# Gated linear attention and a routed MLP: scores in two 64-column halves of the array, several levels per piece

## The chip, the cores and the metric

The kernel runs on one core of one Trainium2 chip. The metric is the device time in microseconds of one execution. All data are fp32 in memory. TensorE (PE) multiplies, PEld is its weight load, DVE is VectorE, ACT is ScalarE, POOL is GpSimd, and SP is the engine whose queue issues most DMAs.

## What is computed

```python
# attention: q, k, v, alpha of shape (4, 8, 768, 48)
for t in range(S):
    state = alpha[:, :, t, :, None] * state + np.einsum('bhd,bhe->bhde', k[:, :, t], v[:, :, t])
    y[:, :, t] = np.einsum('bhd,bhde->bhe', q[:, :, t], state)
# bridge: x = y as (3072, 384); then E = 4 experts, F = 1024
p = domain_probs / (domain_probs.sum(-1, keepdims=True) + 1e-09)
for e in range(E):
    h = np.maximum(x @ w1[e], 0.0)
    out += p[:, e:e + 1] * (h @ w2[e])
```

## The kernel before

**Units and groups.** The 768 steps of a batch row are cut into 6 chunks of 128; a unit is one chunk of one of the 4 batch rows, so there are 24 units. A unit's 128 rows are also 128 tokens of the MLP. Units form seven groups: group 0 has two units, groups 1 to 5 four each, group 6 two. While the MLP of group g runs, the attention of group g+1 is mixed into it, piece by piece; the two units of group 0 run at the start with nothing but filler matmuls (`fill`, L569) beside them.

**A unit of attention** (`attention`, L254) is a generator; each `yield` ends a piece. Pieces 0 to 2 turn alpha, k and q so that head features lie on the partitions, two heads (64 rows each) per tile of 128, four such pairs. The decays between two steps of a chunk are products of alphas; they are applied in seven levels, m = 1, 2, 4, ..., 64. At level m the chunk is cut into blocks of 2m steps, and the scores of keys in the first half of a block with queries in its second half are final. So at each level:

- `next_q` (L290) copies the 64 queries of the second halves to a block `qb` on ACT, two copies, one for each head of a pair, so that the other head's rows of the block stay zero. Then DVE multiplies those queries in QT by the decay of the half before them, and forms the next level's decays `dec`.
- L317: four matmuls, one per pair of heads, with K (128 features x 128 keys) as the stationary operand and `qb` (2 heads x 64 queries) as the moving one. Scores `sc` are 128 keys x 8 heads x 64 queries. From m = 32 on, the last keys are left off (96 and 64 columns).
- L325: DVE multiplies the keys of the first halves, in place in KT, by the decay of the half behind them. As it is in place, it waits until the level's matmuls have read KT.
- the valid part of `sc` goes into `lat`, the unit's 128 x 128 matrix per head: for m up to 16 by a predicated copy on DVE under a mask (L334), for 32 and 64 by three plain copies on ACT (L330).

The diagonal of `lat` is q.k of the same step, written by eight ACT instructions (L272), each a scaled identity. There are two `lat` tiles. Then come `yps` (L352), scores times values plus queries times the old state, on 32 array columns each; the turned K (L369); and the state's update (L373 to L382).

**The MLP.** `up` (L396) computes one of 8 column blocks of 128 of x @ w1; `down` (L454) multiplies one unit's h by w2 in 8 steps. An expert is 8 `up` and then one `down` per unit of the group. Weights come in four pieces (chunks c = 0 to 3) per expert and layer, two `up` per chunk. A weight may be split into three fp32r parts, which multiply faster; the split parts are made once on ACT and DVE (`split_piece`, L199, driven by `background`, L213) and written to DRAM (`kept`), in group 0 for w1 and in group 1 for w2. Later groups load the 1152 KB of a `kept` piece; w1 is unsplit in group 0 (and for chunk 3 of group 6), w2 is unsplit in groups 0, 1 and 6:

```python
    split1 = lambda gi, e, c=0: gi > 0 and (gi < len(groups) - 1 or c < NQ - 1)
    split2 = lambda gi, e, c=0: 1 < gi < len(groups) - 1
```

`load_piece` (L173) issues the load of a piece on SP's queue, which runs in order and waits for the tile to be free. An unsplit piece of 384 KB goes into a `w_raw` tile or into the third part of a `w2` tile. w2 of the next expert is ordered at the end of the last `down` (L503 to L508): two chunks at once and two, `late`, after the first chunk's `up` (L445). `hidden[c]` (L403) is the tile `hT` of a chunk, three parts x 2 column blocks x up to 512 tokens; with unsplit w2 only its third part holds h (L412).

**What sets the order.** The program is written in the order in which each engine runs it. `attend` (L518) gives each unit's pieces a due beat (`BEATS`, L137; units follow one another by 6.5 beats), and `advance` (L538) is called after each `up` and within `down` with an estimated cost (L512), and runs the pieces that are due. For the two units at the start the order is written out by hand (L575, L582).

[...]

## Time and profile before

| | us |
|---|---|
| median of 3 runs | 1161.94 (1161.48 to 1162.81) |
| the profiled execution | 1161.86, of which the span 1160.1 |
| PE busy | 1131.0 (97%) |
| DVE busy | 759.0 (65%) |
| ACT busy | 556.5 (48%) |
| group 0: first `up` to the first of group 1 | 30 to 190 |
| group 6: first `up` to the end | 1078 to 1160 |

HBM reads are 229.8 MB and writes 42.5 MB, 235 GB/s over the span. The granted PE clock is full nearly everywhere after the start. A line of the page such as "x1344 | 180.8, 278 | 16.7" gives the number of instructions, their busy time in us, the mean of one in ns, and the engine's idle time just ahead of them. Matmul records overlap in the pipeline, so the sum of their durations is more than the time that they hold PE; the distance from one start to the next is what counts. An fp32 matmul leaves two matmul records and two weight-load records, an fp32r matmul one of each.

### The profile page before, as it was taken

The numbers are of one execution on the slowest core, as the hardware profiler recorded it, in microseconds if no ns is written. First come the engines' busy times: TensorE is split into PE (matmuls) and PEld (weight loads), VectorE is DVE, ScalarE is ACT, GpSimd is POOL, SyncE is SP. The second block draws the span as 40 slices with busy tenths as digits, with TensorE's granted clock in tenths as the row PEclk, the third lists the DMA queues.
The fourth block names the chain that finished last, engine by engine and source line by source line (L and its number), as shares of the span: only waits on it lengthen the run. The fifth ranks groups of instructions, "written<-read, shape, count | busy, mean of one in ns | idle before, by whom it ended". The sixth has DMA issues, their size and how long they took to land.

```text
span 1160.1 us, 19270 instructions
## 1 busy us (share of the span) xinstructions
PE 1131.0 (97%) x7354; PEld 960.2 (83%) x7354; DVE 759.0 (65%) x1450; ACT 556.5 (48%) x1215; POOL 34.4 (3%) x73
## 2 busy tenths in 40 slices
PE   8789999999999999999999999999999999999998
PEld 8677777686767798998898988989988998998875
DVE  5557755566565868686778695786885777557211
ACT  6557745645636546444456353464462356223221
POOL 1000000000000100000000000000000000000000
PEclk9989999999999999999999999999999999999999
DMA  7657669775767949557749385776493787458783
GB/s 145 215 171 255 203 195 321 263 266 186 251 232 242 395 131 341 170 192 301 263 164 315 127 273 215 258 256 247 132 326 126 294 299 300 169 199 353 236 312 92
DMA packets 166188, 273.54 MB, mean 236 GB/s; under 512 B 120624, under 2 KB 140976, under 8 KB 142032
## 3 DMA queue, kind: packets, MB, share of 16 engines
q1 hardware_dynamic: 156704, 230.06, 57.7%
q0 software_dynamic: 6016, 42.08, 9.1%
q8 instruction: 59, 0.97, 0.3%
q10 hardware_dynamic: 3376, 0.17, 0.2%
q14 instruction: 33, 0.27, 0.1%
HBM read 229.81 MB, written 42.47 MB: 235 GB/s over the span
## 4 chain that ended last, share of the span: by engine, by line
PE 81%; DVE 8%; DMA 4%; ACT 4%; issue 2%; SPq 0%; POOL 0%; ACTq 0%; DVEq 0%; POOLq 0%
PE one L424 17%; PE ops L480 13%; PE sc L317 11%; PE two L424 8%; PE ops L475 7%; PE ops L478 7%; PE ops L476 7%; PE yps L352 4%; PE tp L251 3%; PE one L416 2%; DMA w<-in_moe_w_dram 2%; DVE hT L229 2%; DVE t L430 2%; PE sps L373 1%; DVE hT L233 1%
## 5 line engine op out<-in xcount | busy, mean ns | idle before, releaser
L424 PE MATMUL one<-xT,w 128*128 128x512 f32 (+1 forms) x1104 | 278.5, 387 | 0.9 <-DMA w<-kept 0.9
L424 PEld LDWEIGHTS one<-xT,w 128*128 128x128 f32 x1104 | 191.8, 188 | 37.6 <-issue 2.6
L428 ACT ACTIVATE t<-one 128x512 f32<-128x512 f32 (+1 forms) x184 | 104.9, 570 | 225.6 <-PE one L424 166.8
L317 PEld LDWEIGHTS sc<-qb,KT 128*128 128x128 f32 (+2 forms) x1344 | 168.6, 181 | 44.3 <-ACT qb L297 15.6
L317 PE MATMUL sc<-qb,KT 128*128 128x128 f32 (+2 forms) x1344 | 180.8, 278 | 16.7 <-ACT qb L297 10.1
L475 PE MATMUL ops<-w,hT 128*128 128x384 f32 x512 | 180.7, 353 | 0.0
L297 ACT COPY qb<-QT 64x256 f32<-64x256 f32 x336 | 136.5, 406 | 78.8 <-DVE QT L301 48.2
L478 PE MATMUL ops<-w,hT 128*128 128x384 f32 x512 | 173.1, 338 | 0.4
L476 PE MATMUL ops<-w,hT 128*128 128x384 f32 x512 | 172.6, 337 | 0.0
L424 PE MATMUL two<-xT,w 128*128 128x512 f32 (+1 forms) x552 | 148.6, 377 | 0.0
L480 PE MATMUL ops<-w_raw,hT 128*128 128x384 f32 x384 | 130.8, 487 | 0.0
L325 DVE TENSOR_TENSOR KT<-KT,dec 128x256 f32<-128x256 f32 x144 | 60.8, 422 | 96.3 <-PE sc L317 95.0
L430 DVE TENSOR_TENSOR t<-t,two 128x512 f32<-128x512 f32 x128 | 87.7, 685 | 51.1 <-PE two L424 32.6
L424 PEld LDWEIGHTS two<-xT,w 128*128 128x128 f32 x552 | 100.3, 188 | 19.8
L334 DVE COPY_PREDICATED lat<-masks,sc 128x512 f32<-128x512 uint8 x120 | 113.8, 948 | 0.2
L480 PEld LDWEIGHTS ops<-w_raw,hT 128*128 128x128 f32 x384 | 70.4, 190 | 41.8 <-issue 0.9
L475 PEld LDWEIGHTS ops<-w,hT 128*128 128x128 f32 x512 | 96.3, 188 | 3.3 <-issue 2.8
L478 PEld LDWEIGHTS ops<-w,hT 128*128 128x128 f32 x512 | 96.0, 188 | 2.2 <-DVE hT L233 2.0
L476 PEld LDWEIGHTS ops<-w,hT 128*128 128x128 f32 x512 | 96.4, 188 | 0.2
L233 DVE SCALAR_TENSOR_TENSOR hT<-hT 128x512 fp32r<-128x512 f32 x128 | 88.6, 692 | 4.4
L229 DVE SCALAR_TENSOR_TENSOR hT<-t,hT 128x512 fp32r<-128x512 f32 x128 | 87.6, 684 | 0.0
L226 ACT ACTIVATE hT<-t 128x512 fp32r<-128x512 f32 x128 | 80.3, 627 | 10.4 <-DVE t L430 9.1
(79 smaller groups left out, 1146.3 us busy)
## 6 DMA issues: line engine op xcount, KB each, us to landing
w<-kept SPq DMA_DIRECT2D x156, 1152.0 KB
kept<-w POOLq DMA_DIRECT2D x32, 1152.0 KB, 6.5
w_raw<-in_moe_w_dram SPq DMA_DIRECT2D x32, 384.0 KB
w_raw<-in_moe_w_dram SPq DMA_DIRECT2D x48, 128.0 KB
w<-in_moe_w_dram SPq DMA_DIRECT2D x16, 384.0 KB
ra<-in_alpha_dram SPq DMA_DIRECT2D x23, 192.0 KB
rk<-in_k_dram SPq DMA_DIRECT2D x23, 192.0 KB
rq<-in_q_dram SPq DMA_DIRECT2D x23, 192.0 KB
```

Source lines behind the costliest of these rows:

```text
L229: nc.vector.scalar_tensor_tensor(out=low, in0=x, scalar=0.0, in1=top.bitcast(F32), op0=ALU.max, op1=ALU.subtract)
L233: nc.vector.scalar_tensor_tensor(out=dif, in0=top.bitcast(F32), scalar=1 / 4096.0, in1=low.bitcast(F32), op0=ALU.mult, op1=ALU.subtract)
L297: nc.scalar.copy(out=qb[rows, :, i, :].rearrange("p a (b r) -> p a b r", r=m), in_=qv[rows])
L317: nc.tensor.matmul(sc[:past, 2 * p:2 * p + 2, :].rearrange("p i r -> p (i r)"), lhsT=KT[:, p, :past], rhs=qb[:, p].rearrange("p i r -> p ( ...
L334: nc.vector.copy_predicated(halves(lat, m)[:, :, :, 1, :], mk.unsqueeze(1).broadcast_to([P, H, nb, m]), sc.rearrange("p a (b r) -> p a b r ...
L424: nc.tensor.matmul(out, lhsT=w[:, part, kc], rhs=xTs[gi][:, part, kc, :n], start=(part == terms[0] and kc == 0), stop=(part == terms[-1] a ...
L428: nc.scalar.activation(out=t, in_=one, func=ACT.Copy, scale=FINE)
L430: nc.vector.tensor_sub(t, t, two)
L475: nc.tensor.matmul(sums[0], lhsT=h[:, 1], rhs=w[:, 1], start=(fc == 0), stop=False)
L476: nc.tensor.matmul(sums[0], lhsT=h[:, 0], rhs=w[:, 0], start=False, stop=(fc == FCH - 1))
L478: nc.tensor.matmul(sums[1], lhsT=h[:, 2], rhs=w[:, 2], **ends)
L480: nc.tensor.matmul(sums[0], lhsT=h[:, 2].bitcast(F32), rhs=w, **ends)
```

## The change

Five things are done together.

1. For levels 1 to 32, keys and queries are taken in two halves of 64 steps. Per pair of heads there are two matmuls, each with 64 keys as stationary columns and 2 x 32 queries as moving ones; their outputs lie on partitions 0 to 63 and 64 to 127, so in two halves of the array's columns. Level 64 has keys of the first half and queries of the second alone: four matmuls with 64 stationary and 128 moving columns, two of them in each half of the columns, into `far`.
2. Levels 1 to 8 are multiplied in one piece, levels 16, 32 and 64 in another. For this K of each level has its own tile (five rotate): ACT copies the second halves of the blocks to the new tile, and DVE writes the first halves times the decay. There are four `qb` blocks in place of three.
3. Scores within a half are collected in `near` (128 x 8 x 64), whose diagonal is one DVE product of a stacked identity with `dot` in place of eight ACT instructions. The predicated copies have 32 columns per head in place of 64. Level 32 goes into `near` by two ACT copies, `far` into `lat` by two, `near` into `lat` by two. There is one `lat` tile, whose lower left quarter is zeroed once.
4. An unsplit w2 piece is loaded into the unused first part of its chunk's `hT` tile, ordered when the chunk's first `up` begins; unsplit w1 always goes to the third part of a `w2` tile. The `w_raw` tiles are gone.
5. A unit still has 14 pieces, now at beats 0 to 13, and the order at the start is written anew.

```diff
-    j = np.arange(P)[:, None]
-    n = np.arange(HALF)[None, :]
-    mask_np = np.stack(
-        [(j // (2 * m) == n // m) & (j % (2 * m) < m) for m in LEVELS], 1).astype(np.uint8)
-    ident_np = np.eye(P, dtype=np.float32)
+    j = np.arange(P)[:, None] % HALF
+    n = np.arange(QUAD)[None, :]
+    mask_np = np.stack([(j // (2 * m) == n // m) & (j % (2 * m) < m) for m in LEVELS[:5]],
+                       1).astype(np.uint8)
+    ident_np = np.concatenate([np.eye(P), np.tile(np.eye(HALF), (2, 1))], 1).astype(np.float32)
...
-    ident = const.tile([P, P], F32, name="ident")
-    masks = const.tile([P, len(LEVELS), HALF], U8, name="masks")
+    ident_all = const.tile([P, P + HALF], F32, name="ident")
+    ident = ident_all[:, :P]
+    masks = const.tile([P, 5, QUAD], U8, name="masks")
...
-    lats = [const.tile([P, H, P], F32, name=f"lat{i}") for i in range(2)]
+
+    near = const.tile([P, H, HALF], F32, name="near")
+    lat = const.tile([P, H, P], F32, name="lat")
...
-    blocks = [const.tile([P, NP, 2, HALF], F32, name=f"qb{i}") for i in range(3)]
+    blocks = [const.tile([P, NP, 2, HALF], F32, name=f"qb{i}") for i in range(4)]
...
-    BEATS = [0, 1, 2, 2.5, *range(3, 13)]
+    BEATS = list(range(14))
...
-    def load_piece(l, i):
+    def load_piece(l, i, beside=False):
...
-        if l == 1 and gi == 0 or l == 0 and gi > 0:
+        if l == 1 and not beside:
+            return
+        if l == 0:
+
             w = wts.tile([P, 3, KC * QF], F32R, name="w2", bufs=NQ)[:, 2].bitcast(F32)
         else:
-            w = wts.tile([P, KC * QF], F32, name="w_raw", bufs=NQ)
+
+            w = hidden[c][:, 0].rearrange("p f n -> p (f n)")[:, :KC * QF].bitcast(F32)
         wt[l][i] = w
...
-        lat = lats[u % 2]
         pair = lambda t: lambda p: t[:, 2 * p:2 * p + 2, :].rearrange("p b c -> p (b c)")
+        keys = lambda: work.tile([P, NP, P], F32, name="KT", bufs=5)
 
         AT = work.tile([P, NP, P], F32, name="AT")
-        KT = work.tile([P, NP, P], F32, name="KT")
         QT = work.tile([P, NP, P], F32, name="QT")
         nc.scalar.copy(out=AT, in_=turned(pair(ra)))
-
...
-        def diagonals(which):
-            for h in which:
-                nc.scalar.activation(out=lat[:, h, :], in_=ident, func=ACT.Copy,
-                                     scale=dot[:, h:h + 1])
...
         decs = [AT]
+        KTs = [KT]
+        qbs = []
         spread = lambda t, m: t.unsqueeze(3).broadcast_to([*t.shape, m])
         halved = lambda t: t.rearrange("p a (b two) -> p a b two", two=2)
 
-        def next_q(li):
-
+        def copy_q(li):
             m = LEVELS[li]
             qv = halves(QT, m)[:, :, :, 1, :]
             qb = free.popleft()
+            qbs.append(qb)
             for i in range(2):
                 rows = slice(HD * i, HD * (i + 1))
                 nc.scalar.copy(out=qb[rows, :, i, :].rearrange("p a (b r) -> p a b r", r=m),
                                in_=qv[rows])
-            yield qb
+
+        def next_q(li):
+            m = LEVELS[li]
+            qv = halves(QT, m)[:, :, :, 1, :]
             dv = halved(decs[li])
             nc.vector.tensor_mul(qv, qv, spread(dv[:, :, :, 0], m))
-            dec = work.tile([P, NP, P // (2 * m)], F32, name=f"dec{li}")
+            dec = work.tile([P, NP, P // (2 * m)], F32, name=f"dec{li}", bufs=1)
             nc.vector.tensor_mul(dec, dv[:, :, :, 0], dv[:, :, :, 1])
             decs.append(dec)
 
-        ahead = next_q(0)
-        coming = next(ahead)
-        next(ahead, None)
-        yield
-        for li, m in enumerate(LEVELS):
-            nb = P // (2 * m)
-            qb = coming
-            sc = ps.tile([P, H, HALF], F32, name="sc", tag="sc")
-            wide = m >= 32
-            past = P - m if wide else P
+        def next_k(li):
+            m = LEVELS[li]
+            old = new = halves(KTs[li], m)
+            if li + 1 < len(LEVELS):
+                KTs.append(keys())
+                new = halves(KTs[-1], m)
+                nc.scalar.copy(out=new[:, :, :, 1, :], in_=old[:, :, :, 1, :])
+            nc.vector.tensor_mul(new[:, :, :, 0, :], old[:, :, :, 0, :],
+                                 spread(halved(decs[li])[:, :, :, 1], m))
+
+        def products(li, out):
+
             for p in range(NP):
-                nc.tensor.matmul(sc[:past, 2 * p:2 * p + 2, :].rearrange("p i r -> p (i r)"),
-                                 lhsT=KT[:, p, :past],
-                                 rhs=qb[:, p].rearrange("p i r -> p (i r)"),
+                for s in range(2):
+                    nc.tensor.matmul(
+                        out[HALF * s:HALF * (s + 1), 2 * p:2 * p + 2, :],
+                        lhsT=KTs[li][:, p, HALF * s:HALF * (s + 1)],
+                        rhs=qbs[li][:, p, :, QUAD * s:QUAD * (s + 1)], start=True, stop=True)
+            free.append(qbs[li])
+
+        def take(li, scores):
+            m = LEVELS[li]
+            nb = HALF // (2 * m)
+            mk = masks[:, li, :].rearrange("p (b r) -> p b r", r=m)
+            nc.vector.copy_predicated(
+                near.rearrange("p a (b two r) -> p a b two r", two=2, r=m)[:, :, :, 1, :],
+                mk.unsqueeze(1).broadcast_to([P, H, nb, m]),
+                scores.rearrange("p a (b r) -> p a b r", r=m))
+
+        def scores():
+            return ps.tile([P, 2, H, QUAD], F32, name="sc", tag="sc")
+
+        for li in range(3):
+            copy_q(li)
+            next_q(li)
+            next_k(li)
+            if li == 1:
+
+                nc.vector.tensor_mul(near, ident_all[:, P:].unsqueeze(1).broadcast_to([P, H, HALF]),
+                                     dot.unsqueeze(2).broadcast_to([P, H, HALF]))
+            if li == 2:
+                copy_q(3)
+            yield
+        banks = [scores() for _ in range(2)]
+        for li in range(4):
+            products(li, banks[li // 2][:, li % 2])
+        next_q(3)
+        next_k(3)
+        copy_q(4)
+        take(0, banks[0][:, 0])
+        take(1, banks[0][:, 1])
+        yield
+        next_q(4)
+        next_k(4)
+        copy_q(5)
+        take(2, banks[1][:, 0])
+        take(3, banks[1][:, 1])
+        yield
+        next_q(5)
+        next_k(5)
+        copy_q(6)
+        yield
+        bank = scores()
+        far = ps.tile([P, NP // 2, 2, HALF], F32, name="far", tag="sc")
+        for li in (4, 5):
+            products(li, bank[:, li - 4])
+
+        for r in range(NP // 2):
+            for s in range(2):
+                nc.tensor.matmul(far[HALF * s:HALF * (s + 1), r],
+                                 lhsT=KTs[6][:, 2 * r + s, :HALF], rhs=qbs[6][:, 2 * r + s],
                                  start=True, stop=True)
-            free.append(qb)
-            ahead = next_q(li + 1) if li + 1 < len(LEVELS) else iter(())
-            coming = next(ahead, None)
-            kv = halves(KT, m)[:, :, :, 0, :]
-            nc.vector.tensor_mul(kv, kv, spread(halved(decs[li])[:, :, :, 1], m))
-            if wide:
-
-                for blk in range(nb):
-                    rows = slice(2 * m * blk, 2 * m * blk + m)
-                    nc.scalar.copy(out=lat[rows, :, 2 * m * blk + m:2 * m * (blk + 1)],
-                                   in_=sc[rows, :, m * blk:m * (blk + 1)])
-            else:
-                mk = masks[:, li, :].rearrange("p (b r) -> p b r", r=m)
-                nc.vector.copy_predicated(
-                    halves(lat, m)[:, :, :, 1, :],
-                    mk.unsqueeze(1).broadcast_to([P, H, nb, m]),
-                    sc.rearrange("p a (b r) -> p a b r", r=m))
-            next(ahead, None)
-            yield
+        free.append(qbs[6])
+        next_q(6)
+        next_k(6)
+        take(4, bank[:, 0])
+        for s in range(2):
+            rows = slice(HALF * s, HALF * s + QUAD)
+            nc.scalar.copy(out=near[rows, :, QUAD:], in_=bank[rows, 1])
+        yield
+        parts = lat.rearrange("p (r s i) c -> p r s i c", s=2, i=2)
+        for s in range(2):
+            rows = slice(HALF * s, HALF * (s + 1))
+            nc.scalar.copy(out=parts[:HALF, :, s, :, HALF:], in_=far[rows])
+        for s in range(2):
+            rows = slice(HALF * s, HALF * (s + 1))
+            nc.scalar.copy(out=lat[rows, :, rows], in_=near[rows])
+        KT = KTs[-1]
+        yield
 
...
         if f == 0 and begins:
             hidden[c] = hid.tile([P, 3, FPQ, NT], F32R, name="hT", bufs=NQ)
+            if not split2(gi, e):
+                load_piece(1, i, beside=True)
         if f == 0 and (begins if c < NQ - 1 else ends) and makes[0](*divmod((i + 1) // NQ, E)):
...
+        nc.gpsimd.memset(lat[HALF:, :, :HALF], 0.0)
...
         for i in range(NQ):
             load_piece(0, i)
-        for c in range(NQ):
-            load_piece(1, c)
...
-        for u, n in ((0, 3), (0, 6), (0, 6), (0, 6), (0, 2), (1, 0), (0, 2), (1, 0), (0, 2), (1, 0),
-                     (0, 2), (1, 0), (0, 2), (0, 2), (1, 0), (0, 0), (1, 0), (0, 0)):
+        for u, n in ((0, 3), (0, 6), (0, 4), (0, 6), (0, 6), (0, 6), (1, 0), (0, 2), (0, 2), (1, 2),
+                     (0, 2), (1, 0), (0, 2), (1, 2), (0, 2), (1, 0), (0, 0)):
             next(runs[u])
             fill(n)
         norm_probs()
         making.append(split_piece(0, 0))
 
-        waiting.extend((k, k, runs[u]) for k, u in enumerate((1, 1, 0, 1, 0, 1, 1, 1)))
-        step = 8.5 / (cost(0, 0, 0) * FCH / 2 + cost(1, 0, 0))
+        waiting.extend((k, k, runs[u]) for k, u in enumerate((1, 1, 0, 1, 0, 1, 1, 1, 1)))
+        step = 9.5 / (cost(0, 0, 0) * FCH / 2 + cost(1, 0, 0))
```

## The prediction

> **What bounds the kernel now.** I read first the page's chain of waits and its costliest groups, then the busy time by stage, then the timeline of TensorE (PE) around one unit of attention, then the queue of SP. The chain and the group that the change rewrites:
>
> ```profile
> PE 81%; DVE 8%; DMA 4%; ACT 4%; issue 2%; SPq 0%; POOL 0%; ACTq 0%; DVEq 0%; POOLq 0%
> L317 PE MATMUL sc<-qb,KT 128*128 128x128 f32 (+2 forms) x1344 | 180.8, 278 | 16.7 <-ACT qb L297 10.1
> L334 DVE COPY_PREDICATED lat<-masks,sc 128x512 f32<-128x512 uint8 x120 | 113.8, 948 | 0.2
> L272 ACT ACTIVATE lat<-ident,dot 128x128 f32<-128x128 f32 x192 | 60.9, 390 | 2.0 <-DVE dot L268 1.7
> ```
>
> The score matmuls are 1344 records (672 matmuls, two passes each, in fp32). By stage (columns: stretch, its length, then busy us of PE, PE's weight loads, DVE, ACT, POOL, the granted clock, DMA share, GB/s):
>
> ```profile
> 46.00:166.00 120.00, 109.21 (x802) 85.90 (x802) 74.86 (x159) 70.62 (x166) 5.32 (x10) 0.96 0.66 208
> 188.00:388.00 200.00, 199.05 (x1150) 146.90 (x1150) 123.52 (x228) 114.72 (x234) 11.23 (x21) 1.00 0.72 252
> 388.00:1073.00 685.00, 681.46 (x4601) 614.67 (x4600) 503.17 (x952) 311.73 (x670) 8.11 (x15) 1.00 0.66 242
> 1073.00:1160.00 87.00, 82.84 (x420) 62.99 (x418) 16.26 (x34) 20.81 (x58) 1.08 (x2) 1.00 0.63 213
> ```
>
> From 188 to 1073 us PE is busy 99.5% of the time while DVE stands at 71% and ACT at 48%: PE's own work sets that stretch, and 18 of the 24 units of attention run in it (four in group 1, four in each of groups 2 to 4, two in group 5). Two units run before 46 us, where chains through ACT and DVE decide, and four between 46 and 188 us, where PE is 91% busy up to 166 us. What a score matmul really costs PE is the distance of its starts:
>
> ```profile
> 143.00 0.40 PE L352 MATMUL yps<-lat,rv 128*32 128x128 f32 x8
> 143.22 0.40 PE L352 MATMUL yps<-QT,st 128*32 128x128 f32 x8
> 147.37 1.05 PE L317 MATMUL sc<-qb,KT 128*128 128x128 f32 x8
> 159.57 1.09 PE L317 MATMUL sc<-qb,KT 128*64 128x128 f32 x8
> ```
>
> Eight full-width score records take 1.05 us, and one lasts 0.275, so starts lie (1.05 - 0.275)/7 = 0.11 us apart (0.109 read singly). Eight records of `yps`, which use 32 columns of the array each, follow one another in 0.22 us: 27.5 ns a record with the same 128 moving columns, so four run side by side.
>
> **What the Trainium skill says.** "TensorEngine Tiling (Array Packing)", Key Properties: column tiles load weights and multiply in parallel, and a change of tiling mode drains the array. The trace agrees: eight weight loads of `yps`, 106 ns each, fit in 0.16 us, so they start about 8 ns apart.
>
> ```profile
> 142.75 0.16 PEld L352 LDWEIGHTS yps<-QT,st 128*32 128x32 f32 x8 [0.33 <-issue]
> 159.57 0.85 PEld L317 LDWEIGHTS sc<-qb,KT 128*64 128x64 f32 x8 [0.55 <-ACT lat L330]
> ```
>
> "TensorE: Matmul & The Clock Gate", LDWEIGHTS: the time goes with the columns, columns/1.2 ns, so 53 ns for 64. The first two 64-column loads in the second line start 55 ns apart, the first two 128-column loads of the L480 run behind them 108 ns. The same page, Back-to-back issue gap, gives a floor of about 25 ns between starts; `yps` starts within a burst of four are only 7 ns apart, so I don't use it as a limit. No run of before has two 64-column tiles at once.
>
> **The change part by part.**
>
> 1. Score matmuls. Before, a unit has 7 levels x 4 matmuls x 2 records = 56 records x 109.2 ns = 6.12 us. After, levels 1 to 32 have 8 matmuls each, with 64 array columns and 64 moving columns; each half gets 6 x 4 x 2 = 48 records of 128/2.4 = 53 ns (half of the 109 less its 2.5 ns) + 2.5 = 55.8 ns, and the weight load of 53 to 55 ns fits behind it: 2.68 us. Level 64 has per half 2 matmuls x 2 records x 109.2 = 0.44 us. Sum 3.11 us, a saving of 3.0 us a unit if the halves run side by side. Bounds: if they don't, 96 x 55.8 + 8 x 109.2 = 6.2 us, no gain. I take 3.0.
>
> 2. Changes of array mode. Leaving `yps` costs about 0.2 us (a gap of 0.1 and a score group of 1.16 instead of 1.05 us), entering 0.1. After, a unit enters a tiled mode for two score groups and `yps`; before for level 64 (the 64-column form) and `yps`. One more round trip, +0.3 us; against it five fewer score groups squeezed between fp32r matmuls, each of which costs 0.05 to 0.08 us at its entry. I take 0, with +-0.3 us x 18 = 5 us for the range.
>
> 3. ACT, per unit: 8 diagonals x 0.39 and 3 `lat` copies x 0.434 go (-4.4 us); six K copies (x ~0.41, by the 64x256 row of L297 at 406 ns), two `near`, two `far` and two `lat` copies come (+2.5 + 0.87 + 0.8 + 1.2): +0.9 us, 21 us in all on an engine at 48%. DVE: five predicated copies on half the elements (-5 x 0.45), one `near` product (+0.69 by L279's 685 ns): -1.6 us, 37 us in all. Both lie beside PE, which needs no result of a level before the next piece; cost 0. If that cover went, at most a few of these copies per unit would show.
>
> 4. PE's waits for `qb` and K. The view of line L317 gives 25.8 us of idle before it until an ACT `qb` copy (weight loads and matmuls together, so partly twice), nearly all before 166 us. With levels 1 to 8 multiplied together, from blocks and K tiles made a piece earlier, and K no longer multiplied in place, most such waits go. In 46 to 166 us PE idles 10.8 us; I take 5 back, and of the four units' 12 us of matmul 9, since SP's queue is nearly full there: -14 us.
>
> 5. The first 46 us: the seven levels of unit 0 are a chain of ACT (0.81 for Q, 0.42 for K) and DVE (0.43 + 0.19 to 0.42 + 0.42) at about 1.4 us a level, plus about 4 us for taking scores; `yps` comes near 28 us as now (28.6). Cost 0, +-3.
>
> 6. w2 of the groups without split w2 (0, 1 and 6) now goes into part 0 of the chunk's own `hT` tile, and its load is issued at that chunk's first `up` instead of one expert ahead. On SP it stands behind the w1 loads of the chunks before it, and SP waits in order. The lines that matter:
>
> ```profile
> 171.59 0.34 SPq L181 DMA_DIRECT2D w<-kept  x1
> 182.97 0.33 SPq L181 DMA_DIRECT2D w<-kept  x1
> 191.77 0.32 SPq L181 DMA_DIRECT2D w<-kept  x1
> ...
> 1079.95 4.56 SPq L181 DMA_DIRECT2D w<-kept  x3
> ```
>
> In group 0's last expert SP holds at each of these `kept` loads until a split piece has been written out. Chunk 3's w2 is queued behind the second (182.97) and lands near 188; `down`, begun at 177.4, wants it at 181.4: +6 us. In group 6 `up` lasts 8.8 us and `down` wants chunk 3 after 3.9 more, at 12.5; queued ahead from about 2 us on are two pieces of 1152 KB (2.7 us each at the 422 GB/s of 1082 to 1090 us) and chunk 2's 384 KB, then its own (about 2 us each at the 184 GB/s of 1096 to 1098), done near 14: +1.5 us x 4 experts = +6. In group 1 a chunk takes about 5 us and its slack is 10, enough; its start may be later by +1. Bounds for all twelve experts: 0 to 5 us each. I take +13 in sum.
>
> Sum: 18 units x 3.0 = -54; -14; +13; = -55. The profiled execution took 1161.86 us (span 1160.1, 1.8 outside), the median is 1161.94, so they are the same to 0.1. 1162 - 55 = 1107.
>
> **Rivals.**
>
> - The halves take turns, because weight loads of two 64-column tiles are serialized: `yps` could not show this, its loads being only 27 ns each at 27.5 ns a record. Then 6.2 us a unit as before; the place is every score group, the price 3.0 us a unit, and it decides as soon as the starts of records in a group lie about 55 ns apart instead of 28. With +13 for w2 and -8 for waits: 1167, slower. Against it: the eight loads in 0.16 us. 8%.
> - w2 is late at most of the twelve experts (3 to 5 us each, 36 to 60 us): 1162 - 68 + 48 = 1142. For it: SP's queue is issuing nearly without a pause from 60 to 106 us, and attention loads hold it 8 to 11 us at a time; against it: group 0's experts last 25 to 40 us, so slack is large but for the last. 14%.
> - PE's gain isn't all on the path from 188 us on, DVE or a transfer of 1152 KB ending later instead: half of 54 lost, 1134. Against it: DVE loses work, and DMA share 0.66 leaves room. 8%.
> - More than forecast: the waits of group 0 go wholly and w2 costs nothing: 1162 - 54 - 22 = 1086. 12%.
>
> **How the numbers follow.** Forecast 1107, with 58%, its own range 1094 to 1122. To leave out no more than 2 in 10 the range takes in half the late-w2 case and most of the better one: 1088 to 1138. A measurement of this kernel tells 0.2% (2.3 us) from no change. Slower: the turns rival and a far worse w2, 9%; within 0.2%, 2%; faster 89%.
>
> **What would show it.** Score records in a group should start in pairs, some 56 ns from pair to pair, and a unit's 104 records take some 3.1 us; 55 ns between single records would make the forecast wrong. Idle PE before L540 (the later line of `down`'s unsplit matmuls) until a DMA should stand at 6 us in group 0's last expert and about 1.5 in each of group 6; much more, or any in group 1, would show the late-w2 case. Idle before the score matmuls until `qb` should be under 10 us. DVE should lose about 37 us and ACT gain about 21.

## The result, and the profile after

The kernel after takes 1173.96 us (median of 4 runs, 1170.63 to 1176.31), the kernel before beside it 1162.38 us (1161.48 to 1163.22). The ratio is 1.0098, 95% interval 1.0069 to 1.0126: one per cent slower, where 1107 was forecast. The profiled execution took 1176.31 us, its span is 1174.5.

First the page of after: the chain of waits, and the groups that answer to those shown of before.

```profile
PE 66%; DVE 14%; DMA 8%; ACT 8%; issue 3%; SPq 1%; ACTq 0%; DVEq 0%
L323 PE MATMUL sc<-qb,KT 128*64 128x64 f32 x2304 | 80.7, 227 | 3.7 <-ACT qb L297 3.7
L540 PE MATMUL ops<-hT 128*128 128x384 f32 x512 | 182.2, 504 | 20.1 <-DMA hT<-in_moe_w_dram 19.3
L484 PEld LDWEIGHTS one<-xT,w 128*128 128x128 f32 x1104 | 194.2, 188 | 50.8 <-ACT t L488 11.9
L535 PE MATMUL ops<-w,hT 128*128 128x384 f32 x512 | 179.6, 351 | 13.0 <-ACT t L488 9.9
L297 ACT COPY qb<-QT 64x256 f32<-64x256 f32 x336 | 137.2, 408 | 130.3 <-DVE QT L304 103.9
```

Before, PE held 81% of the chain, now 66%; DVE, DMA and ACT have taken the difference. The scores themselves are cheap: 80.7 us of records (and 15.9 for `far`) where there were 180.8, and only 3.7 us of waiting for `qb`. What is new stands in the next rows. Unsplit `down` (L540) waits 19.3 us for a load of w2, and PE waits for the eviction `t` of the MLP's own `up` product, ACT's copy of it out of PSUM, where PE has summed it (L488), which no row of the page of before names. ACT in turn sits 103.9 us idle before `qb` until DVE has multiplied the queries. In before, unsplit `down` waited for nothing, and ACT's wait for DVE was 48.2 us:

```profile
L480 PE MATMUL ops<-w_raw,hT 128*128 128x384 f32 x384 | 130.8, 487 | 0.0
L297 ACT COPY qb<-QT 64x256 f32<-64x256 f32 x336 | 136.5, 406 | 78.8 <-DVE QT L301 48.2
```

By stage (columns as in the table of before: stretch, length, busy us of PE, weight loads, DVE, ACT, POOL, granted clock, DMA share, GB/s):

```profile
166.00:210.00 44.00, 30.10 (x165) 20.96 (x158) 13.47 (x20) 11.12 (x22) 2.15 (x4) 0.81 0.65 212
210.00:388.00 178.00, 178.00 (x1300) 128.57 (x1299) 109.01 (x216) 115.02 (x226) 8.02 (x15) 1.00 0.71 247
388.00:1073.00 685.00, 655.75 (x5240) 569.44 (x5239) 490.25 (x963) 329.88 (x691) 9.72 (x18) 0.99 0.66 241
1073.00:1174.00 101.00, 94.95 (x490) 75.27 (x488) 24.69 (x50) 23.34 (x64) 2.17 (x4) 1.00 0.62 222
```

From 388 to 1073 us PE was busy 681.46 of 685 us before; now it is 655.75, so 29 us are idle. Taken from the first `up` of each group to that of the next (group 6 to PE's last matmul), in us:

| group | 0 | 1 | 2 | 3 | 4 | 5 | 6 |
|---|---|---|---|---|---|---|---|
| before | 159.4 | 197.5 | 179.9 | 180.7 | 177.3 | 152.6 | 78.8 |
| after less before | +22.5 | -13.7 | -3.9 | +3.7 | +3.2 | +2.3 | +2.1 |
| forecast | -8 | -11 | -12 | -12 | -12 | -6 | +6 |

Only group 1 does what was forecast. Groups 2 to 5 miss 47 us (+5.3 in place of -42), group 0 misses 30. Two different things happen in these two places.

**Group 0, the last expert.** The timeline of PE, then of SP's queue, in after:

```profile
180.59 2.74 PE L540 MATMUL ops<-hT 128*128 128x384 f32 x8
...
188.59 2.93 PE L540 MATMUL ops<-hT 128*128 128x384 f32 x4 [5.25 <-DMA hT<-in_moe_w_dram]
200.94 6.83 PE L540 MATMUL ops<-hT 128*128 128x384 f32 x12 [8.57 <-DMA hT<-in_moe_w_dram]
```

```profile
175.34 0.34 SPq L184 DMA_DIRECT2D w<-kept  x1
175.73 0.42 SPq L202 DMA_DIRECT2D hT<-in_moe_w_dram  x1
190.04 0.34 SPq L184 DMA_DIRECT2D w<-kept  x1
190.43 0.43 SPq L202 DMA_DIRECT2D hT<-in_moe_w_dram  x1
```

The bracket is PE's idle time ahead of the row and what ended it. SP issues the load of a chunk's w2 (L202) only after a `kept` load of w1 (L184), which it holds until that piece has been written. Chunk 2's load is issued at 175.73 us, right behind a `kept` load of 1152 KB, and PE gets it at 188.59. Chunk 3's has to wait for the next `kept` load, which SP holds for 13.6 us, until 190.04; PE gets it at 200.94. So `down` of this expert stops twice, 5.25 and 8.57 us, and it is slow behind a stop: four records take 2.93 us at 188.59, where eight took 2.74 at 180.59. The granted clock of this stretch is 0.81; in the kernel before it was 1.00 from 165 to 190 us, where the same `down` ran.

**Groups 2 to 5, one `up` phase.** The last `up` of an expert in group 3, PE, then DVE, then ACT:

```profile
640.30 1.56 PE L484 MATMUL one<-xT,w 128*128 128x512 f32 x6
641.70 0.85 PE L484 MATMUL two<-xT,w 128*128 128x512 f32 x3
645.29 0.44 PE L535 MATMUL ops<-w,hT 128*128 128x384 f32 x1 [2.75 <-ACT t L488]
```

```profile
640.70 0.68 DVE L490 TENSOR_TENSOR t<-t,two 128x512 f32<-128x512 f32 x1
641.30 0.69 DVE L236 SCALAR_TENSOR_TENSOR hT<-t,hT 128x512 fp32r<-128x512 f32 x1
642.02 0.69 DVE L240 SCALAR_TENSOR_TENSOR hT<-hT 128x512 fp32r<-128x512 f32 x1
642.63 0.42 DVE L304 TENSOR_TENSOR QT<-QT,dec 128x256 f32<-128x256 f32 x1
...
643.37 0.42 DVE L333 COPY_PREDICATED near<-masks,sc 128x256 f32<-128x256 uint8 x1
```

```profile
643.88 0.74 ACT L387 COPY near<-sc 32x256 f32<-32x256 f32 x2 [3.21 <-DVE near L333]
644.64 0.60 ACT L488 ACTIVATE t<-one 128x512 f32<-128x512 f32 x1
```

PE has finished `one` near 641.9 us, but ACT evicts it at 644.64. ACT isn't busy: it stands 3.21 us at the level-32 copy, an attention instruction ahead in its order, until DVE has done its predicated copy; and DVE comes to that copy late, behind the splitting of h and three attention products. One column block of `up` costs DVE three passes of 0.68 to 0.69 us, 2.06 us, while PE needs about 2.2 us for its nine matmuls (starts 638.13 to 640.30). So next to a bare `up` DVE has little room, and what an attention piece asks of DVE comes on top.

DVE isn't full over these phases, though. The sums over the 16 `up` phases of groups 2 to 5, before and then after (length, then busy us of each engine):

```profile
sum 341.20, PE 340.19 PEld 283.10 DVE 283.31 ACT 199.77 POOL 2.17; mean PE 21.26 PEld 17.69 DVE 17.71 ACT 12.49 POOL 0.14
sum 345.60, PE 326.32 PEld 262.23 DVE 265.69 ACT 183.76 POOL 2.94; mean PE 20.39 PEld 16.39 DVE 16.61 ACT 11.48 POOL 0.18
```

PE idles 19.3 us of them where it idled 1.0, while DVE's share is 77%, less than the 83% of before. What stops PE is the waiting of ACT and DVE for each other in their orders, not a DVE that is busy all the time.

### The profile page after: what moved, and what is told of

Same layout as the page of the kernel before. It is cut to its first block, busy times and chain, and to the rows that moved or that the text cites. A ratio compares the mean times of both kernels' runs of the same rounds, so it can differ in the third digit from the quotient of the medians.

```text
span 1174.5 us, 21708 instructions
## 1 busy us (share of the span) xinstructions
PE 1093.9 (93%) x8530; PEld 900.8 (77%) x8530; DVE 734.8 (63%) x1474; ACT 586.0 (50%) x1239; POOL 35.5 (3%) x75
## 4 chain that ended last, share of the span: by engine, by line
PE 66%; DVE 14%; DMA 8%; ACT 8%; issue 3%; SPq 1%; ACTq 0%; DVEq 0%
PE one L484 13%; PE ops L540 12%; PE ops L535 7%; PE ops L538 7%; PE ops L536 6%; PE two L484 6%; DMA hT<-in_moe_w_dram 4%; PE sc L323 4%; PE yps L410 4%; DVE hT L236 3%; DVE t L490 3%; PE tp L258 2%; DVE hT L240 2%; ACT t L488 2%; ACT qb L297 2%
## 5 line engine op out<-in xcount | busy, mean ns | idle before, releaser
L484 PEld LDWEIGHTS one<-xT,w 128*128 128x128 f32 x1104 | 194.2, 188 | 50.8 <-ACT t L488 11.9
L488 ACT ACTIVATE t<-one 128x512 f32<-128x512 f32 (+1 forms) x184 | 105.0, 571 | 202.5 <-PE one L484 149.6
L297 ACT COPY qb<-QT 64x256 f32<-64x256 f32 x336 | 137.2, 408 | 130.3 <-DVE QT L304 103.9
L540 PE MATMUL ops<-hT 128*128 128x384 f32 x512 | 182.2, 504 | 20.1 <-DMA hT<-in_moe_w_dram 19.3
L540 PEld LDWEIGHTS ops<-hT 128*128 128x128 f32 x512 | 96.3, 195 | 83.4 <-issue 15.3
L323 PEld LDWEIGHTS sc<-qb,KT 128*64 128x64 f32 x2304 | 73.2, 140 | 21.7 <-issue 14.0
L323 PE MATMUL sc<-qb,KT 128*64 128x64 f32 x2304 | 80.7, 227 | 3.7 <-ACT qb L297 3.7
L304 DVE TENSOR_TENSOR QT<-QT,dec 128x256 f32<-128x256 f32 x144 | 60.5, 420 | 32.3 <-ACT qb L297 31.8
L493 DVE TENSOR_TENSOR hT<-t,two 128x512 f32<-128x512 f32 (+1 forms) x56 | 32.1, 573 | 69.2 <-ACT t L488 50.7
```

Source lines behind the costliest of these rows:

```text
L297: nc.scalar.copy(out=qb[rows, :, i, :].rearrange("p a (b r) -> p a b r", r=m), in_=qv[rows])
L323: nc.tensor.matmul(out[HALF * s:HALF * (s + 1), 2 * p:2 * p + 2, :], lhsT=KTs[li][:, p, HALF * s:HALF * (s + 1)], rhs=qbs[li][:, p, :, QUA ...
L484: nc.tensor.matmul(out, lhsT=w[:, part, kc], rhs=xTs[gi][:, part, kc, :n], start=(part == terms[0] and kc == 0), stop=(part == terms[-1] a ...
L488: nc.scalar.activation(out=t, in_=one, func=ACT.Copy, scale=FINE)
L540: nc.tensor.matmul(sums[0], lhsT=h[:, 2].bitcast(F32), rhs=w, **ends)
```

## The experiments

Two theories stood at first: that the loads of w2 are late, and that the copies of `qb` and `near` stand wrongly in the order of ACT and DVE. A third, that DVE is full during `up`, came from the first round.

### w2 ordered early, and copies a piece later

e1 orders the four loads of the next expert's w2, with their `hT` tiles, at the end of the last `down`:

```diff
-            hidden[c] = hid.tile([P, 3, FPQ, NT], F32R, name="hT", bufs=NQ)
-            if not split2(gi, e):
-                load_piece(1, i, beside=True)
+            chunk_tile(gi, e, c)
...
+            then = divmod(gi * E + e + 1, E)
+            if then[0] < len(groups) and not split2(*then):
+                for c in range(NQ):
+                    chunk_tile(*then, c)
```

> The changed kernel, but the four w2 loads of the next expert are ordered at the end of the last down (as before), still into the hT tile. Theory W+O (the gain of 3.0 us a unit is real and is eaten by late w2 in groups 0 and 6 and by ACT waiting in its queue for DVE): PE idle until a DMA before the unsplit down (19.3 us in the changed kernel) falls under 4 us, the slowed clock around 182 to 210 us goes with it, and the time falls by 20 to 30 us to 1144 to 1154. Rival W alone (w2 is all of the loss): 1105 to 1115. Rival 'the halves don't bring 3 us': 1144 to 1154 too, but then no further fall in e3.

Measured: 1169.49 us (1167.12 to 1173.73), ratio 1.0065 [1.0043, 1.0087]. A miss. Group 0 fell from 181.9 to 165.6 us, as the theory wants, but group 1 rose by 8 and groups 5 and 6 by 5.5: with four loads of w2 ahead of w1 on the queue, PE's `up` now waited for w1 (7.3 us for `kept` pieces, 3.6 for unsplit ones).

e2 moves each ACT copy of queries to the piece after the DVE product that makes them, and the level-32 copies to the piece after the last predicated copy; a unit has 16 pieces. The `near` product stays where it was, in a unit's second level. With 16 pieces it comes before the last reading of `near` by the unit ahead, so that some scores are overwritten in e2 and e3; every instruction is still there.

```diff
         for li in range(3):
             copy_q(li)
+            next_k(li)
             next_q(li)
-            next_k(li)
             if li == 1:
                 nc.vector.tensor_mul(near, ...)
-            if li == 2:
-                copy_q(3)
             yield
+        copy_q(3)
+        yield
...
-        next_q(3)
         next_k(3)
-        copy_q(4)
...
+        next_q(3)
         yield
+        copy_q(4)
```

> The changed kernel, but each qb copy stands at the start of the piece after the one in which DVE makes its queries, the near copies a piece after the predicated copy, K before Q on DVE; 16 pieces instead of 14. w2 as in the change. Theory W+O: groups 2 to 5 fall from 696 us to 650 to 660, ACT's idle until DVE QT (104 us) falls under 40, the time is 1125 to 1140. Rival W alone: no change in groups 2 to 5, 1170 to 1178.

Measured: 1173.59 us (1171.66 to 1178.31), ratio 1.011 [1.0079, 1.014]. ACT's idle time before `qb` fell from 103.9 to 34.2 us, and the time didn't move: groups 2 to 5 took 694.8 us in sum against 695.8. PE now waited for `lat` instead, six times and 19.0 us in these groups. The trace shows why. One of the six, ACT and then PE:

```profile
464.91 0.75 ACT L387 COPY near<-sc 32x256 f32<-32x256 f32 x2 [2.83 <-DVE near L346]
467.64 0.65 PE L409 MATMUL yps<-lat,rv 128*32 128x128 f32 x8 [3.77 <-ACT lat L394]
```

L346 is the `near` product of the next unit. Ahead of each of the six stops ACT's level-32 copy has waited for it, 0.95 to 2.83 us, 12.5 us in all. So this wait comes with the product that was left in its place. PE idles 26.3 us in groups 2 to 5 of e2, and 19.0 of them are these six stops; the other 7.3 stand against 29.3 in after. The later copies did take away PE's waits for `t`, then, and a fault of this version put new ones there. What the order alone is worth at the change's own pace, e2 doesn't tell; that it is worth nothing it doesn't show.

e3 is both edits.

> Both of the edits of e1 and e2. Theory W+O: the forecast of 1107 comes back, 1100 to 1118. If something else costs as much, 1130 or more.

Measured: 1173.69 us (1172.1 to 1177.98), ratio 1.011 [1.0081, 1.0139]. A miss again, and with the same fault: here too PE waits 19.0 us for `lat` in groups 2 to 5.

### Part 4 alone, in the kernel before

e4 puts the load of unsplit w2 into the `hT` tile, at the chunk's first `up`, and unsplit w1 into the third part of a `w2` tile; it changes nothing else of before.

```diff
-            w = wts.tile([P, KC * QF], F32, name="w_raw", bufs=NQ)
+            w = hidden[c][:, 0].rearrange("p f n -> p (f n)")[:, :KC * QF].bitcast(F32)
...
+            if not split2(gi, e):
+                load_piece(1, i, beside=True)
```

> The kernel before with part 4 of the change alone: unsplit w2 into the hT tile, ordered at the chunk's first up; w1 to the w2 tile. Theory W: group 0's last expert and group 6 stall as in the change, 1175 to 1190, with 12 to 20 us of PE idle until a DMA before line L480's successor. Rival (w2 is late only because PE comes earlier in the changed kernel): within 5 us of before.

Measured: 1184.88 us (1182.41 to 1189.07), ratio 1.0204 [1.0167, 1.024]. Group 0 took 179.3 us (159.4 before), group 6 83.5 (78.8), and all others stayed within 1.2 us. The row of unsplit `down` in e4:

```profile
L484 PE MATMUL ops<-hT 128*128 128x384 f32 x512 | 187.8, 507 | 20.4 <-DMA hT<-in_moe_w_dram 20.4
```

The wait is that of after (19.3 us), without any change of attention. So part 4 costs about 22 us by itself, and the rest of the change gains about 11 (1184.88 - 1173.96).

### The pace: attention out of the `up` phases

`advance` runs the pieces that are due by an estimated cost. e7 changes one number of after, which in groups 2 to 5 counts an `up` at 0.6 in place of 2.1, so that most pieces fall into `down`; e8 does the same in before.

```diff
-            return 2.1 * n if split1(gi, e) else 2.6 * n
+            return 0.6 * n if split2(gi, e) else 2.1 * n if split1(gi, e) else 2.6 * n
```

> The changed kernel, with one number changed: in groups 2 to 5 an up counts as 0.6 instead of 2.1 us for the pace of the attention pieces, so that most of them run in the down phases, where DVE is idle for a third. Theory U (in the up phases DVE has 2.06 us of splitting for 2.08 us of PE, so attention's DVE work there stops PE as soon as PE's own share of attention shrinks): groups 2 to 5 fall from 696 us to 655 to 670, the time to 1135 to 1150. Rival Q (a wait inside the unit, whichever phase it is in: ACT copies behind DVE products of the same piece): no fall or up to 10 us.

> Control: the kernel before with the same shift of the pieces into the down phases. It is PE-bound at 99.5 percent there, so theory U expects no gain: 1158 to 1166, or a loss where a down phase gets too dense. If the shift alone brings 10 us or more here, it says nothing about the change.

Measured: e7 1146.26 us (1144.98 to 1146.79), ratio 0.9871 [0.9856, 0.9886], groups 2 to 5 down from 695.8 to 664.1 us. e8 1164.02 us (1161.36 to 1167.03, 15 runs), ratio 1.003 [1.0021, 1.0039]. The same number is worth some 27 us in after; in before the time is 3 us longer with it, and groups 2 to 5 are 2.4 us shorter. One expert of group 3, its `up` phase and then its `down` phase, in after, in before, and in e7:

```profile
617.50:645.30 27.80, 23.50 (x199) 18.58 (x197) 20.08 (x42) 12.87 (x27) 0.00 (x0) 1.00 0.87 303
645.30:671.70 26.40, 25.31 (x245) 23.62 (x246) 19.27 (x43) 14.07 (x32) 0.00 (x0) 0.94 0.24 80
```

```profile
613.70:637.10 23.40, 23.40 (x132) 19.74 (x131) 20.09 (x41) 16.45 (x37) 0.00 (x0) 1.00 0.93 328
637.10:661.90 24.80, 24.80 (x216) 24.24 (x214) 18.70 (x40) 6.62 (x15) 0.00 (x0) 1.00 0.36 111
```

```profile
615.80:634.10 18.30, 18.30 (x114) 14.65 (x113) 13.86 (x26) 11.20 (x23) 0.00 (x0) 1.00 0.97 384
634.10:662.00 27.90, 27.79 (x354) 25.80 (x354) 22.33 (x53) 17.00 (x40) 0.00 (x0) 1.00 0.54 177
```

In this `up` phase of before PE is never idle, with DVE at 20.09 of 23.40 us. After has the same DVE work there, 20.08 us, and the same PE work, 23.50; but the phase takes 27.80 us and PE idles 4.3 of it. In e7 DVE has 13.86 us there, and PE is busy throughout. That the spread and longer scores of before covered the waits of ACT and DVE fits this, but no run shows it by itself.

### DVE's work taken away

e10 leaves out one of the three DVE passes that split h (its third part, wherever w2 is split); the third matmul reads the second part instead. So PE's work stays, and 0.69 us of DVE per `up` goes. e11 is the same in before.

```diff
+        if not relu:
             nc.vector.scalar_tensor_tensor(out=dif, in0=top.bitcast(F32), ...)
...
-                nc.tensor.matmul(sums[1], lhsT=h[:, 2], rhs=w[:, 2], **ends)
+                nc.tensor.matmul(sums[1], lhsT=h[:, 1], rhs=w[:, 2], **ends)
```

> The changed kernel without the third part of h: DVE leaves out its last product per up in groups 2 to 5 (0.69 us of 2.06), and the third matmul of down reads the second part instead, so the output is not the reference's. Pace and order as in the change. Theory U: the up phases get the slack on DVE that they lack, groups 2 to 5 fall from 696 to 650 to 665 us, the time to 1130 to 1145. Rival Q (ACT's place in the order, whatever DVE's load): 685 us or more.

> Control: the kernel before without the third part of h, in the same way. Theory U: PE sets the stretch there, so taking 88 us from DVE brings at most 5 us.

Measured: e10 1138.63 us (1136.99 to 1139.6), ratio 0.9799 [0.9776, 0.9822], groups 2 to 5 at 661.4 us, 34.4 less than after. e11 1155.02 us (1153.54 to 1155.36), ratio 0.9943 [0.9923, 0.9962], 6.5 us less than before in groups 2 to 5, a little more than the 5 allowed. Two edits that have little in common, less DVE work and attention placed elsewhere, give the same 32 to 34 us in after and 2 to 7 in before. e7 moves ACT's and PE's share of the pieces too; e10 touches DVE's work alone. So how much DVE has to do sets how long PE waits in after, and hardly in before. It doesn't follow that DVE is full there.

### Versions with the causes mended

e5 is e7 with w2 ordered early, two loads at the end of the last `down` and two after the first chunk's `up`, as the kernel before has it. e6 is e5 with e2's order of copies, but with the `near` product moved to the first taking of scores and a unit's last three pieces half a beat later, so that units keep clear of each other's `near`. e9 is e6 with the K copies on POOL. e12 is e6 with an `up` counted at 1.2 in place of 0.6.

```diff
e5, at the end of the last `down`:
+                if c >= NQ // 2:
+                    late.append(k)
+                else:
+                    chunk_tile(*divmod(k // NQ, E), c)
e6:
-    BEATS = list(range(14))
+    BEATS = [*range(13), 13.5, 14.5, 15.5]
e9:
-                nc.scalar.copy(out=new[:, :, :, 1, :], in_=old[:, :, :, 1, :])
+                nc.gpsimd.tensor_copy(out=new[:, :, :, 1, :], in_=old[:, :, :, 1, :])
e12:
-            return 0.6 * n if split2(gi, e) else ...
+            return 1.2 * n if split2(gi, e) else ...
```

> As e7_shift_alone, and the w2 loads ordered as before the change (two at the end of the last down, two after the first chunk's up). Theory U with late w2: 20 us less than e7_shift_alone, 1115 to 1130. Rival Q: 1160 to 1170.

> As e5_shift_w2_early, and the qb and near copies a piece later, the near product beside the first predicated copies, 16 pieces. If ACT's waits for DVE in the same piece cost much in the down phases too: 5 to 15 us under e5. If not: the same within 4 us.

> As e6_shift_w2_copies, with the six copies of K per unit on POOL instead of ACT. If ACT's queue is what keeps group 0 at 163 us (PE waits there for lat, K and x copies, some 20 us): group 0 falls by 5 to 10 us, the time to 1118 to 1124. If POOL's copies are slow or hold DVE up: slower than 1128.

> As e6_shift_w2_copies, with 1.2 in place of 0.6 for an up in groups 2 to 5. Theory U: between no shift (2.1) and 0.6, groups 2 to 5 at 668 to 685 us; 1131 to 1148.

| | us | ratio to before | group 0 | groups 2 to 5 |
|---|---|---|---|---|
| e5 | 1131.97 (1131.12 to 1133.37) | 0.9751 [0.9736, 0.9765] | 164.8 | 664.3 |
| e6 | 1128.08 (1125.87 to 1129.78) | 0.971 [0.9693, 0.9726] | 162.7 | 665.3 |
| e9 | 1130.04 (1128.55 to 1131.33) | 0.973 [0.9709, 0.9751] | 161.9 | 666.2 |
| e12 | 1116.56 (1115.49 to 1118.0) | 0.9615 [0.9595, 0.9635] | 162.0 | 656.3 |

Early w2 is worth 14 us (e5 against e7): 14 in group 0 and 4.8 in group 6, less 4.5 in group 1. The order of the copies adds 4 us, none of it in groups 2 to 5, and POOL's copies gain nothing. The result of e12, better than expected, shows that 0.6 had been too far. The same two phases of group 3 in e12:

```profile
595.50:614.20 18.70, 18.70 (x118) 15.23 (x117) 17.25 (x37) 13.49 (x30) 0.00 (x0) 1.00 0.95 342
614.20:639.70 25.50, 25.50 (x289) 24.24 (x288) 20.34 (x47) 13.41 (x30) 0.00 (x0) 1.00 0.70 230
```

PE is busy for the whole of both, 44.2 us for the expert against 54.2 in after and 48.2 in before. The sum over the 16 `up` phases of groups 2 to 5 in e12:

```profile
sum 304.20, PE 303.74 PEld 248.18 DVE 256.10 ACT 173.48 POOL 2.16; mean PE 18.98 PEld 15.51 DVE 16.01 ACT 10.84 POOL 0.13
```

DVE's share is 84% here, higher than the 77% of after, and PE idles 0.5 us. With pace and order set together, an `up` phase carries this much DVE work without stopping PE.

e15 asks how much of that is the order: e12 with the copies where the change had put them.

> The kernel after with w2's loads ordered early and an `up` of groups 2 to 5 counted at 1.2 us, but with a unit's copies where the change put them: tells how much of the best version's time is the order of the copies and how much the two other edits. Theory: the order is worth 0 to 6 us, as with 0.6 in place of 1.2, where it was 4; so 1116 to 1123. Rival: at this pace the order decides, 1126 to 1134.

Measured: 1138.82 us (1137.75 to 1140.31), ratio 0.9805 [0.9783, 0.9827], groups 2 to 5 at 672.5 us. The rival was right, and by more than it said: at this pace the order is worth some 20 us (22 against e12, 20 against e17 below), where it was worth 4 with 0.6 (e6 against e5). Of the 22 us, 16 lie in groups 2 to 5 and 5 in group 0. ACT's row in e15, then in e12:

```profile
L297 ACT COPY qb<-QT 64x256 f32<-64x256 f32 x336 | 137.0, 408 | 123.8 <-DVE QT L304 97.9
```

```profile
L297 ACT COPY qb<-QT 64x256 f32<-64x256 f32 x336 | 136.8, 407 | 83.9 <-DVE QT L304 37.0
```

With the change's order each ACT copy waits for a DVE product of the same piece, and the evictions of `up` queue behind it. What the later copies, with the `near` product later too, would bring at the change's own pace wasn't run.

### Group 0

Even in e12 group 0 takes 162 us against 159.4 before, with PE's busy time there down from 143.6 to 137.4 us. e13 counts an `up` of group 0 at 1.0 instead of 2.6 in e12, e14 in before.

```diff
-            return ... else 2.6 * n
+            return ... else (1.0 if gi == 0 else 2.6) * n
```

> e12 with one more number: in group 0 an `up` counts 1.0 instead of 2.6 us for the pace of attention, so that more of group 1's attention runs inside group 0's `down` phases. Theory (in group 0's `up` phases ACT is full, since w1 is split there, and PE waits for its copies of K, qb, near and lat): group 0 falls from 162 to 147 to 157 us, the time to 1100 to 1112. Rival (the waits are each unit's own chain, wherever it runs): group 0 stays at 160 to 164, the time at 1114 to 1119.

> The kernel before with the same number in group 0 alone, the control for it. Theory: less to gain, since its levels are single and PE's longer scores cover the splitting: group 0 159.4 us before, 155 to 162 here, the time within 4 us of before. If it gains as much as the other, group 0's pace was wrong in the kernel before already and has nothing to do with the change.

Measured: e13 1123.07 us (1116.11 to 1123.9), ratio 0.9654 [0.9622, 0.9687], group 0 at 167.5 us in place of 162.0. e14 1163.8 us (1160.1 to 1166.79), ratio 1.0023 [1.0013, 1.0033]. The theory fell: pace is not the cure here. PE's waits from 28 to 188 us in before and 28 to 190 in e12 (us in total, times, longest):

```profile
PE sc L317 <- ACT qb L297: 8.7, 6, 3.7
PE sps L373 <- ACT AT L369: 3.5, 2, 2.8
```

```profile
PE yps L408 <- ACT lat L393: 10.3, 4, 4.9
PE sps L429 <- ACT AT L425: 4.8, 2, 4.1
PE sc L323 <- ACT qb L297: 3.2, 3, 2.0
PE far L376 <- ACT qb L297: 2.3, 3, 1.0
```

The waits for `qb` fall from 8.7 to 5.5 us, and a wait for `lat` that before hadn't is as long as what they were. Its copies on ACT, in e12:

```profile
91.61 0.84 ACT L211 ACTIVATE w<-w 128x768 fp32r<-128x768 f32 x1 [1.26 <-DMA w<-in_moe_w_dram]
92.36 0.73 ACT L386 COPY near<-sc 32x256 f32<-32x256 f32 x2
93.12 0.75 ACT L390 COPY lat<-far 64x256 f32<-64x256 f32 x2
93.77 1.25 ACT L393 COPY lat<-near 64x512 f32<-64x512 f32 x2
```

Six copies, 2.7 us, stand at a unit's end behind the splitting of w1, where before the diagonals and most levels had been in `lat` long since. The splitting itself (L211) has stood 1.26 us here, until a load of w1 came, and the six copies with it. e16 is e12 with the last two on DVE for the four units that run beside group 0; e17 is e12 itself, on the same chip.

```diff
-            nc.scalar.copy(out=lat[rows, :, rows], in_=near[rows])
+            if 2 <= u < 6:
+                nc.vector.tensor_copy(out=lat[rows, :, rows], in_=near[rows])
+            else:
+                nc.scalar.copy(out=lat[rows, :, rows], in_=near[rows])
```

> e12 with the two copies from near to lat (2 x 0.62 us on ACT) moved to DVE for the four units whose attention runs beside group 0's MLP. Theory: the new wait of group 0 is ACT in line: PE's `yps` waits for lat 10.3 us (4 stretches) because near, far and lat copies, 2.7 us, stand behind the copies and splits on ACT, where the kernel before had no such wait; with 1.25 us of each unit's 2.7 gone from ACT, the wait falls to 3 to 6 us, group 0 from 162 to 156 to 160, the time to 1111 to 1117. Rival: the wait is that of the scores themselves (DVE's masked copies end late); then it only changes its name, and group 0 stays at 161 to 165.

> e12 once more, unchanged, on the same chip as the run above, so that a few microseconds between the two can be told: 1114 to 1120 expected.

Measured: e16 1116.44 us (1113.12 to 1119.61), e17 1118.61 us (1116.38 to 1119.04); their ranges overlap, so the time tells nothing. In the one profiled execution of each, group 0 is 159.1 us in e16 against 161.9 in e17, and the wait for `lat` 8.1 against 12.0 (10.3 in e12, which is the same kernel). So some 2 to 4 us of the wait go, and the larger part stays. What the rest waits for wasn't tried further.

## Why the prediction was wrong

**Step 1, the scores: the mechanism right, the size too large.** 3.0 us a unit was forecast, from 6.12 to 3.11. The timeline of after has the second and third score group of a unit:

```profile
636.48 1.15 PE L323 MATMUL sc<-qb,KT 128*64 128x64 f32 x32
637.51 0.66 PE L378 MATMUL far<-qb,KT 128*64 128x128 f32 x8
```

32 records in 1.15 us, each lasting about 0.22: (1.15 - 0.22) / 31 = 30 ns a record, not 55. Read singly they start in pairs, 8 ns apart in a pair and 59 from pair to pair. The halves run side by side, as "TensorEngine Tiling (Array Packing)", Key Properties, has it; the rival in which they take turns is out. But from the first start of a group to the start of what follows it, a unit's score groups hold PE for 5.85 us before and 3.54 after (medians over groups 1 to 5): 2.3 us less, not 3.0. A full-width group of before gives PE back 0.03 us after its last record has started, where the sum counted 0.11. The tiled groups of after hold it 0.15 us (levels 1 to 8) and 0.20 us (`far`) after theirs. Step 2 had set such ends at nothing, against 0.05 to 0.08 us at the entry of each full-width group; but there the starts lie 0.18 or 0.23 us apart, as they do between the fp32r matmuls themselves. For the 14 units of groups 2 to 5 this makes 10 of the 47 us that are missing.

**Step 3 failed, and with it the sum.** It said of ACT and DVE: "Both lie beside PE, which needs no result of a level before the next piece; cost 0." That is so for the scores. But PE also needs ACT to evict each `up` product and DVE to split it, and these stand in the same two orders as the attention pieces, behind copies and products that wait for each other. In groups 2 to 5 PE stood idle for 29.3 us in after, 19.3 of it in the `up` phases, where it had stood 3.5 before, and its clock was halved for a while behind some of the stops. The ground for cost 0 was averages, DVE 71% and ACT 48% from 188 to 1073 us. They hide two kinds of phases, with DVE at 83% in `up`; and no engine has to be full for PE to wait.

What shows this: e7 and e10, which place attention's work elsewhere or leave out some of DVE's, give 32 and 34 us back in groups 2 to 5, and their controls e8 and e11 show that before had hardly any of this cost. e15 and e12 differ in the order and beats of a unit's pieces alone, and e12 is 16 us shorter there. How much the order alone would have given at the change's own pace is open (e2 points to a good part). The third rival named DVE as a later end, but at half of the gain and 8%; in these groups the waits took all of it. With pace and order mended (e12), PE idles 3.3 us in groups 2 to 5, and they stand 34.2 us below before. That is what 14 units at 2.3 us give (32), so nothing of step 1's real gain is lost there any more.

The sizes in step 3 were better than its conclusion: DVE lost 24 us (759.0 to 734.8; 37 forecast), ACT gained 29.5 (556.5 to 586.0; 21 forecast).

**Step 6: the mechanism right, mis-sized.** It named the queue, the place and the expert, with +6 us for group 0. The two stops were 5.25 and 8.57 us, the stretch from 166 to 210 us ran at a clock of 0.81, and part 4 alone cost group 0 19.9 us and the kernel 22 (e4). It priced the wait for chunk 3 and not the one for chunk 2, and took no price for PE's clock after a stop. In group 6 it said +6: 4.7 in e4. In group 1, no wait was forecast and none came.

**Step 4: half right.** The waits for `qb` in group 0 fell from 8.7 us to 5.5 in e12 (6.8 in after up to 166 us), and the 2.0 us of waits for K went: about the 5 that it took back. But the 9 us of the shorter scores (4 units at 2.3) are matched by the new wait for `lat` (10.3), which the step didn't look for: it asked which wait goes, not which is late next.

Step 5 is not contradicted by anything above: the start is 1.8 us shorter than before, within the 3 allowed.

## What to carry to other kernels

An average busy share over a long stretch hides alternating phases, and even the share of a phase doesn't tell whether an engine will be late: with DVE at 77% PE lost 19 us, with DVE at 84% and another order and pace it lost 0.5. Ask of each phase what the engine on the path needs from the others, and what stands ahead of that in their orders. When work is interleaved by estimated costs, a change that shortens one engine's part makes the old estimates wrong, and pace and order must be set again together: pace alone gave 27 us; pace and order, with the earlier loads of w2, turned +1.0% into -3.9%. A test of order must move everything that shares a tile: one product left in its place hid what the order was worth. A load that moves to a later place on an in-order queue pays for everything that is held ahead of it, at its worst place.

## What the hardware showed unexpectedly

- The end of a score group in tiled mode costs more than that of a full-width one: the next instruction starts 0.15 us (`sc`) or 0.20 us (`far`) after the last record has started, against 0.03 us. Between `sc` and `far`, both on 64 columns, it is 0.05 us.
- A stop of PE costs more than its length. Between 178 and 210 us of after, with stops of 5.25 and 8.57 us, the mean granted clock was 0.73. "TensorE: Matmul & The Clock Gate", What's actually happening, has the clock fall after about 3.4 us idle; both stops are longer, and the trace agrees. But in the `down` of group 3 shown above, behind a stop of only 2.75 us, the clock was halved for 3.4 us (0.94 in the mean of that `down`), so here a shorter stop was enough.
- POOL takes 514 ns for a K copy of 128x256, in e9; ACT takes 416 in e6:

```profile
L315 POOL COPY KT<-KT 128x256 f32<-128x256 f32 x144 | 73.6, 514 | 671.0 <-DVE KT L316 233.5 <-ACT KT L276 166.1 <-PE tp L258 119.6
```

- DVE copies 64x512 from `near` to `lat` in 0.42 us where ACT takes 0.62 (e16).
